# Two linked feed-forward layers after attention: the groups of the first layer alternate between two parts of the tokens, and its weights are used for both parts from one load

## The chip, the cores and the metric

The kernel is one program on one core of a Trainium2 chip. The metric is the time of one execution on the device in microseconds (us). TensorE does the matrix products, VectorE, ScalarE and GpSimd the work on single elements, and SyncE (with ScalarE's queue) starts the transfers between HBM and the on-chip memory. In the profile these engines are PE, DVE, ACT, POOL and SP; PEld is TensorE's loading of weights, and ACTq and SPq are transfers that ScalarE and SyncE start.

## The reference

```python
B, H, S, D = 4, 8, 576, 64                # 2304 tokens of 512 columns after attention
# attention with a causal softmax, mixed by a gate with a linear memory (not touched by the change)
x = attn_out.transpose(0, 2, 1, 3).reshape(B * S, H * D)
h = x @ moe_w_in                          # 512 -> 2048
x = np.maximum(0.01 * h, h) @ moe_w_out   # 2048 -> 512
a, b = x @ moe2_w_a, x @ moe2_w_b         # 512 -> 1536, twice
out = (a * b) @ moe2_w_out                # 1536 -> 512
```

All inputs and the result are 32-bit floats, and the weights reach the kernel as 64-bit words that it turns into 32-bit values by integer and float operations on VectorE.

## The kernel before

**Products.** Each matrix factor is kept as a high and a low half (`hi`, `lo`, two tiles of reduced-precision floats whose sum is the value), and each product is made of three matmuls: hi·hi, hi·lo and lo·hi (`three`, lines 393 to 395). The common unit is a matmul of 128x128 weights with 512 columns.

**The first layer.** The 2304 tokens are in two parts: part 0 has 1024 (two chunks of 512 columns), part 1 has 1280 (chunks of 512, 512 and 256). The 2048 hidden columns are in eight groups of 256. For a group g, `inward` computes the hidden values: for each chunk and each half f of the group a block of 12 matmuls into a bank of PSUM (ring `u`, four banks), then ScalarE applies the leaky ReLU into a buffer `gf` (line 1099) and casts it to the high half of a gate tile (1063), and GpSimd subtracts to get the low half (1064). `outward` multiplies the gate tiles of a set of groups with the output weights, four blocks per chunk (ring `o`, four banks); for the first set ScalarE copies the result to the running sum `xf` (line 1115), for later sets VectorE adds it (line 1117). A set of one group has 6 matmuls in a block of `outward`, a set of two has 12.

**The order of the sets.** Group 0 is done for both parts, then the sets [1,2], [3,4], [5,6], [7] of part 0, and then [1,2], [3,4], [5], [6,7] of part 1. All engines run in the order in which the program is written; `after(k, ...)` puts an operation k blocks later, `tick` counts the blocks.

**Weights.** The class `Weights` converts 68 items of 512 columns: 32 "own" items (two for each of the 16 weight tiles of the first layer), then 24 "plain" items and 12 "last" items of the second layer. Four own items are done during attention, 64 during the first layer. An item is loaded by SyncE (`wraw`, line 178), ScalarE takes the absolute value (line 261), VectorE does the steps of lines 292, 293, 302, 303, 307, and for an own item ScalarE casts the high half (299) and VectorE makes the low half (314, 315); a plain or last item ends with one sum (322 or 330) and is written to HBM by SyncE. `convert` sets the pace: so many quarters of an item for each block of matmuls. Converted tiles live in five slots (`RING`). Part 0 uses each tile once and frees it; each own tile is therefore also written to HBM (`kept`, line 318, started by ScalarE) and 14 are read back for part 1 (line 361, started by ScalarE).

**The last 256 tokens of part 1** as halves (`xt`) lie in the tile that later holds a gate; they are written to HBM once (`xkept`) and read back once.

**The second layer** (`moe2`) makes its products from sums of blocks with seven products (1, 6, 5, 7, 2, 3, 4 in `slots`) instead of eight, and `result` (line 1421) multiplies with the output weights and lets VectorE add. At the end of part 0 the sums of part 1's input (`Sums.jobs`, lines 1177 and 1189) are made between the last products.

Of the kernel before, what the change touches and what calls it, by code (L numbers as in the profile page):

```python
# [11 lines left out]
F32 = mybir.dt.float32  # L12
# [105 lines left out]
def attention_moe_moe2(ctx: ExitStack, tc, kqT, qn, vn, m_prev, beta, w_in, w_out, w_a, w_b, w_o2, out):  # L118
# [38 lines left out]
    class Weights:  # L157


        def __init__(self, first, ab, last):  # L160
            self.sources = {"own": first, "plain": ab, "last": last}
            self.pool = None
            self.own = self.n = self.top = self.quarter = self.freed = self.got = 0
# [94 lines left out]
        def absolute(self, n):  # L258

            t = self.abs[n] = {x: self.temp(n, [P, WC], F32, "w" + x) for x in "har"}  # L260
            nc.scalar.activation(t["h"], self.raw[n][:, :, 1].bitcast(F32), AF.Abs)  # L261
# [22 lines left out]
        def quarters(self, n, item):  # L284
# [25 lines left out]
            def four():  # L310
                if n + 1 in self.items:
                    self.absolute(n + 1)
                if kind == "own":
                    V.tensor_tensor(t["a"], t["a"], f32(self.tiles[i][:, 0, c]), ALU.subtract)
                    V.tensor_tensor(self.tiles[i][:, 1, c], t["a"], t["h"], ALU.add)  # L315
                    if part:
                        w = f32(self.tiles[i]).rearrange("p s c -> p (s c)")
                        after(2, lambda: nc.scalar.dma_start(self.kept[i], w))
                    self.done.add(item)
                elif kind == "plain":  # L320
                    k = "p (k f c) -> p f k c"
                    V.tensor_tensor(
                        t["r"].rearrange("p (f k c) -> p f k c", f=2, k=2), t["a"].rearrange(k, k=2, f=2),
                        t["h"].rearrange(k, k=2, f=2), ALU.add,
                    )

                    nc.sync.dma_start(self.plain[i][:, part], t["r"])
                    self.done.add(item)
                else:
                    V.tensor_tensor(t["r"], t["a"], t["h"], ALU.add)  # L330
                    nc.sync.dma_start(self.saved[i][:, part], t["r"])
# [18 lines left out]
        def get(self):  # L350
            i = self.got
            if i < 16:
                self.until("own", i)
            self.got += 3 if i == 15 else 1
            return self.tiles.pop(i)
# [8 lines left out]
        def free(self):  # L364
            self.freed += 3 if self.freed == 15 else 1
            self.fetch()
# [11 lines left out]
    FIRST_SETS = [[1, 2], [3, 4], [5, 6], [7]]  # L378
# [741 lines left out]
    def moe1(ps, pr, sets, x, y):  # L1120
        for groups in sets:
# [5 lines left out]
            for g in groups:  # L1127
                weights.free()
# [499 lines left out]
```

## Time and profile before

| what | value |
| --- | --- |
| time, median of 3 runs | 1033.75 us (1029.85, 1033.75, 1033.86) |
| profiled execution | 1029.21 us, span 1027.4 us, mean granted clock 0.992 |
| PE busy | 997.3 us, 97% of the span |
| DVE busy | 805.7 us, 78% |
| ACT busy | 422.3 us, 41% |
| POOL busy | 402.7 us, 39% |
| HBM read and written | 111.15 MB and 55.05 MB |

Attention ends at about 195 us after the start of the span, the first layer at about 588 us, and the second layer's part 0 at about 790 us. A busy PE includes the time in which a matmul is only draining, so the place to look for lost time is where the step from one matmul's start to the next grows.

### The profile page before, as it was taken

The page shows a single profiled execution, that of the slowest core. Times are in us where ns is not written, and L with a number is a line of the kernel's source. Part 1 is how long each engine was busy: PE and PEld are TensorE (multiplying, and loading weights), DVE is VectorE, ACT ScalarE, POOL GpSimd, SP SyncE. Part 2 cuts the span into 40 slices and gives each one's busy share as a digit, 9 for nine tenths or more (in the row PEclk, how much of TensorE's full clock was granted, in tenths as well). Part 3 has the DMA queues.
Part 4 walks back from the last instruction along what each step waited for, and adds up shares of the span by engine and source line. Part 5 has one row for each costly group of instructions (what it writes and reads, how often), then busy time and mean ns, then how long its engine had stood idle before and what let it go on. Part 6 is the DMA issues. An engine that isn't in the chain of part 4 may idle for free.

```text
span 1027.4 us, 14691 instructions
## 1 busy us (share of the span) xinstructions
PE 997.3 (97%) x5266; PEld 800.8 (78%) x5266; DVE 805.7 (78%) x1520; ACT 422.3 (41%) x947; POOL 402.7 (39%) x371
## 2 busy tenths in 40 slices
PE   9999999999999899999999999999997999999998
PEld 4666667787878688788888878878875888888887
DVE  6999998698999989799987396797787627647646
ACT  7988886665342422415134144332232222201201
POOL 6787777333141412505034366766643101001000
PEclk9999999999999899999999999999998999999999
DMA  7334531155446468667673235456564432332312
GB/s 235 107 119 137 169 114 48 63 171 207 175 163 224 160 206 314 223 211 260 209 262 103 103 123 215 161 199 225 202 215 156 144 133 93 137 141 93 140 46 103
DMA packets 49273, 167.16 MB, mean 163 GB/s; under 512 B 5168, under 2 KB 12080, under 8 KB 40752
## 3 DMA queue, kind: packets, MB, share of 16 engines
q1 hardware_dynamic: 45024, 136.86, 38.9%
q10 hardware_dynamic: 4176, 29.37, 7.7%
q8 instruction: 41, 0.67, 0.3%
q14 instruction: 32, 0.26, 0.1%
HBM read 111.15 MB, written 55.05 MB: 162 GB/s over the span
## 4 chain that ended last, share of the span: by engine, by line
PE 70%; DVE 21%; DMA 5%; ACT 2%; issue 2%; POOL 0%; ACTq 0%; DVEq 0%; SPq 0%; POOLq 0%
PE b L393 19%; PE b L395 19%; PE b L394 19%; PE b L744 4%; PE b L823 4%; PE b L685 3%; DMA wraw<-in_w_b 3%; DVE wh L292 2%; DVE wa L302 2%; DVE w L315 2%; DVE wh L307 2%; DVE xf L1117 2%; DVE wh L303 1%; PE b L795 1%; DVE xs L1189 1%
## 5 line engine op out<-in xcount | busy, mean ns | idle before, releaser
L1359 DVE TENSOR_TENSOR gf<-b,gf 128x512 f32<-128x512 f32 x168 | 114.2, 687 | 72.0 <-PE b L395 67.3
L1421 DVE TENSOR_TENSOR xf<-b,xf 128x512 f32<-128x512 f32 (+1 forms) x91 | 61.8, 682 | 61.7 <-PE b L395 61.5
L375 POOL TENSOR_TENSOR w<-w 128x512 fp32r<-128x512 f32 x24 | 35.3, 1471 | 188.6 <-ACT w L374 188.2
L1064 POOL TENSOR_TENSOR hl<-gf,hl 128x512 fp32r<-128x512 f32 (+1 forms) x37 | 53.3, 1454 | 136.9 <-ACT hl L1063 125.7
L393 PE MATMUL b<-xh,w 128*128 128x512 f32 x256 | 101.7, 397 | 2.4 <-ACT gf L1099 2.4
L394 PE MATMUL b<-xh,w 128*128 128x512 f32 x256 | 100.5, 392 | 0.0
L395 PE MATMUL b<-xh,w 128*128 128x512 f32 x256 | 100.2, 392 | 0.0
L261 ACT ACTIVATE wh<-wraw 128x512 f32<-128x512 f32 x64 | 42.9, 671 | 97.4 <-DMA wraw<-in_w_o 32.4
L393 PE MATMUL b<-xs,bhi 128*128 128x512 f32 (+1 forms) x216 | 79.4, 368 | 2.7 <-DVE gf L1359 2.7
L393 PE MATMUL b<-xs,ahi 128*128 128x512 f32 (+1 forms) x216 | 79.1, 366 | 1.6 <-DVE gf L1359 1.6
L394 PE MATMUL b<-xs,bhi 128*128 128x512 f32 (+1 forms) x216 | 79.2, 367 | 0.2 <-DVE xs L1189 0.2
L394 PE MATMUL b<-xs,ahi 128*128 128x512 f32 (+1 forms) x216 | 79.0, 366 | 0.0
L395 PE MATMUL b<-xs,blo 128*128 128x512 f32 (+1 forms) x216 | 79.0, 366 | 0.0
L395 PE MATMUL b<-xs,alo 128*128 128x512 f32 (+1 forms) x216 | 78.9, 365 | 0.0
L639 ACT ACTIVATE p<-p,stat 128x512 f32<-128x512 f32 (+3 forms) x128 | 71.0, 559 | 5.3 <-DVE stat L693 4.9
L1117 DVE TENSOR_TENSOR xf<-b,xf 128x512 f32<-128x512 f32 (+1 forms) x80 | 50.1, 630 | 25.0 <-PE b L395 25.0
L666 POOL TENSOR_SCALAR p<-p,stat,keep 128x128 f32<-128x128 f32 (+3 forms) x95 | 61.0, 655 | 16.9 <-DVE stat L654 8.6
L1064 POOL TENSOR_TENSOR qs<-gf,qs 128x512 fp32r<-128x512 f32 (+1 forms) x21 | 28.8, 1370 | 92.7 <-ACT qs L1063 72.0
L393 PE MATMUL b<-w,hl 128*128 128x512 f32 (+1 forms) x146 | 57.1, 391 | 7.6 <-DVE xf L1421 7.6
L693 DVE CUSTOM_DVE_ANT_0 p<-b,mask 128x512 f32<-128x512 f32 (+3 forms) x128 | 57.4, 477 | 6.1 <-PE b L685 5.6
L393 PE MATMUL b<-hl,w 128*128 128x512 f32 (+1 forms) x164 | 61.6, 375 | 0.1
L394 PE MATMUL b<-hl,w 128*128 128x512 f32 (+1 forms) x164 | 61.3, 374 | 0.0
(201 smaller groups left out, 2726.1 us busy)
## 6 DMA issues: line engine op xcount, KB each, us to landing
kept<-w ACTq DMA_DIRECT2D x14, 1024.0 KB, 4.3
w<-kept ACTq DMA_DIRECT2D x14, 1024.0 KB, 5.3
wraw<-in_w_in SPq DMA_DIRECT2D x16, 512.0 KB, 3.6
wraw<-in_w_out SPq DMA_DIRECT2D x16, 512.0 KB, 3.7
qraw<-in_qn SPq DMA_DIRECT2D x8, 768.0 KB, 6.9
wraw<-in_w_b SPq DMA_DIRECT2D x12, 512.0 KB, 4.3
plain<-wr SPq DMA_DIRECT2D x24, 256.0 KB, 4.6
wraw<-in_w_a SPq DMA_DIRECT2D x12, 512.0 KB, 5.3
```

Source lines behind the costliest of these rows:

```text
L261: nc.scalar.activation(t["h"], self.raw[n][:, :, 1].bitcast(F32), AF.Abs)
L393: nc.tensor.matmul(outp, l_hi, r_hi, start=start, stop=False)
L394: nc.tensor.matmul(outp, l_hi, r_lo, start=False, stop=False)
L395: nc.tensor.matmul(outp, l_lo, r_hi, start=False, stop=stop)
L639: nc.scalar.activation(t, t, AF.Exp, bias=s[:, 0, col : col + 1], scale=-1.0, accum_out=s[:, 1, col : col + 1])
L666: ENG[eng].tensor_scalar(live[p], live[p], stats[w % 3][:, 3, col : col + 1], k, ALU.mult, ALU.mult)
L693: nc.vector.tensor_tensor_reduce(one(p, [P, wd]), plan.tiles[banks[j]][:, c : c + wd], mask[:, off : off + wd], -0.125, BIG, ALU.add, ALU. ...
L744: nc.tensor.transpose(tt[0:kw, n * 128 : n * 128 + 128], live[name][:, kt * 128 : kt * 128 + kw], ident)
L1064: after(1 if eng is nc.vector else 2, lambda: eng.tensor_tensor(t[:, 1, c], gf, f32(t)[:, 0, c], ALU.subtract))
L1117: nc.vector.tensor_tensor(y[:, dm, c], op[:, 0:n], y[:, dm, c], ALU.add)
L1359: nc.vector.tensor_tensor(left[q, to], src, left[q, add], ALU.add)
L1421: nc.vector.tensor_tensor(y[:, i, c], op, y[:, i, c], ALU.add)
```

## The change

The sets become one list, `SETS`, in which parts alternate and each part lags or leads by one group: part 0 [0], part 1 [0,1], part 0 [1,2], part 1 [2,3], part 0 [3,4], part 1 [4,5], part 0 [5,6], part 0 [7], part 1 [6,7]. A weight tile stays in its slot until both parts have used it (`used`), so nothing of it is written to HBM or read back. Part 1 has four sets instead of five. In `inward` the low half for f = 1 is made by VectorE instead of GpSimd, with the number of operations the same. The fourth gate tile of a part-1 set holds the last 256 tokens' halves in its first 1024 columns until the set's second group has used them (its chunks come in the order 2, 0, 1), so these are read back from `xkept` at the start of the sets 3, 5 and 8. The plain and last items are summed in place (`wa`), in plain order; the second layer takes its blocks from that order (`columns`, `pair`). In `slots`, the last column pair of part 0 gets the same mixed order as the others, and four sums of part 1's input are put behind its last product.

```diff
-            self.kept = [dram.tile([P, 4 * WC], F32, tag=f"kept{i}", name=f"kept{i}") for i in range(16)]
...
                     V.tensor_tensor(self.tiles[i][:, 1, c], t["a"], t["h"], ALU.add)
-                    if part:
-                        w = f32(self.tiles[i]).rearrange("p s c -> p (s c)")
-                        after(2, lambda: nc.scalar.dma_start(self.kept[i], w))
                     self.done.add(item)
                 elif kind == "plain":
...
-                    nc.sync.dma_start(self.plain[i][:, part], t["r"])
+                    V.tensor_tensor(t["a"], t["a"], t["h"], ALU.add)
+                    nc.sync.dma_start(self.plain[i][:, part], t["a"])
...
-        def fetch(self):
-            while self.asked < min(32, self.freed + RING):
-                i = self.asked
-                t = f32(self.tile(i)).rearrange("p s c -> p (s c)")
-                after(2, lambda t=t, i=i: nc.scalar.dma_start(t, self.kept[self.again[i - 18]]))
-                self.asked += 1
...
+        def used(self, i):
+            self.uses[i] += 1
+            if self.uses[i] == 2:
+                self.tiles.pop(i)
+                self.freed = i + 1
...
-    FIRST_SETS = [[1, 2], [3, 4], [5, 6], [7]]
-    SECOND_SETS = [[1, 2], [3, 4], [5], [6, 7]]
+    SETS = [(0, [0]), (1, [0, 1]), (0, [1, 2]), (1, [2, 3]), (0, [3, 4]), (1, [4, 5]), (0, [5, 6]), (0, [7]), (1, [6, 7])]
...
-                halves(t, c, gf, nc.gpsimd)
+                halves(t, c, gf, nc.vector if f else nc.gpsimd)
...
+    def moe1(ps, first, fourth, x, y):
+        for n, (pr, groups) in enumerate(SETS):
             gt = []
+            t3 = fourth(n) if pr or len(groups) > 1 else None
+            for j, g in enumerate(groups):
+                if n == 0:
+                    gt += first
+                else:
+                    ts = [shared("qs0"), t3] if j else [shared("hl0"), shared("hl1")]
+                    gt += ts
+                    cs = chunks(pr)
+                    wi = weights.get(2 * g)
+                    for kind, w in inward(ps, pr, g, wi, x[pr], ts, cs[2:] + cs[:2] if j else cs):
+                        yield n, kind, g, w
+                weights.used(2 * g)
+            wos = [weights.get(2 * g + 1) for g in groups]
+            for kind, w in outward(ps, pr, groups[-1], wos, gt, y(pr), n < 2):
+                yield n, kind, groups[-1], w
...
-                text = ("16572O3O4OO", "1657234OOOO" if g == 5 else "1O6O5OO7234")[a] if g else "1657234"
+                text = ("16572O3O4OO", "1O6O5OO7234")[a] if g else "1657234"
...
+                if n > 1:
+                    nc.sync.dma_start(f32(t)[:, :, 0:1024], xkept)
...
+            convert(w, 0.7 if n == 0 else 0.74)
...
-                jobs += [steps[x] for x in {"1": "1b", "6": "6", "5": "5", "7": "7c", "2": "2", "3": "3", "4": "4"}[k]]
+                jobs += [steps[x] for x in {"1": "1b", "6": "6", "5": "5", "4": "7c234"}.get(k, "")]
```

How the order of instructions moves, at three places. The first is ScalarE where part 1 follows part 0, before: the names are a gate tile (`qs`, `xs`), `gf` the leaky ReLU, `wh` the absolute value of a loaded item, `w<-kept` a weight read back.

```order
L1099 ACTIVATE gf_4391<-b_4378 128x512
L261 ACTIVATE wh<-wraw 128x512
L361 DMA w<-kept_76 128x2048
L361 DMA w<-kept_77 128x2048
L361 DMA w<-kept_78 128x2048
L1063 CAST qs_4377<-gf_4391 128x512
L1099 ACTIVATE gf_4421<-b_4408 128x512
L1063 CAST xs_4275<-gf_4421 128x512
L1099 ACTIVATE gf_4442<-b_4429 128x512
L261 ACTIVATE wh<-wraw 128x512
L1063 CAST qs_4377<-gf_4442 128x512
```

And ScalarE at the start of a part-1 set now (`hl` is a gate tile, lines 1077 and 1043 are the leaky ReLU and the cast).

```order
L1077 ACTIVATE gf_4489<-b_4476 128x512
L261 ACTIVATE wh<-wraw 128x512
L1043 CAST hl_4474<-gf_4489 128x512
L1077 ACTIVATE gf_4512<-b_4499 128x512
L1043 CAST hl_4475<-gf_4512 128x512
L1077 ACTIVATE gf_4535<-b_4522 128x512
L261 ACTIVATE wh<-wraw 128x512
L1043 CAST hl_4474<-gf_4535 128x512
```

No transfer is started by ScalarE any more; the waits for loaded items (line 261) still stand ahead of the leaky ReLUs. The second place is VectorE in the `inward` part of the set 3 now: one plain item and the subtraction that GpSimd did before (line 1044).

```order
L292 TENSOR_SCALAR wh<-wh 128x512
L293 TENSOR_SCALAR wa<-wh 128x512
L302 SCALAR_TENSOR_TENSOR wa<-wraw,wa 128x512
L303 TENSOR_SCALAR wh<-wa 128x512
L307 SCALAR_TENSOR_TENSOR wh<-wraw,wh 128x512
L1044 TENSOR_TENSOR hl_3618<-gf_3655,hl_3618 128x512
L318 TENSOR_TENSOR wa<-wa,wh 128x512
```

Each item of about two blocks now has one such subtraction in the middle of it. The third place is VectorE at the end of the second layer's part 0, from product 3 of the last pair on. Before:

```order
L1359 TENSOR_TENSOR gf<-b_7422,gf 128x512
L1386 TENSOR_TENSOR gf<-gf 128x512
L1177 TENSOR_TENSOR raw<-xf,raw 128x512 x2
L1359 TENSOR_TENSOR gf<-b_7435,gf 128x512
L1386 TENSOR_TENSOR gf<-gf 128x512
L1344 TENSOR_TENSOR hl_7400<-gf,hl_7400 128x512
L1421 TENSOR_TENSOR xf<-b_7452,xf 128x512
L1189 TENSOR_TENSOR xs_4275<-raw,xs_4275 128x512 x2
L1421 TENSOR_TENSOR xf<-b_7465,xf 128x512
```

And now, from the first product's sum on (1419 is the addition of an output block, 1357 a sum of products, 1384 the product of the two columns, 1342 the low half of a gate, 1166 and 1178 the sums of part 1's input and their low halves).

```order
L1419 TENSOR_TENSOR xf<-b_7225,xf 128x512
L1166 TENSOR_TENSOR raw<-xf 128x512 x2
L1357 TENSOR_TENSOR gf<-b_7235,gf 128x512
L1178 TENSOR_TENSOR xs_5890<-raw,xs_5890 128x512 x2
L1419 TENSOR_TENSOR xf<-b_7247,xf 128x512
L1357 TENSOR_TENSOR gf<-b_7255,gf 128x512
L1178 TENSOR_TENSOR xs_5890<-xf,xs_5890 128x512 x2
L1419 TENSOR_TENSOR xf<-b_7267,xf 128x512
L1419 TENSOR_TENSOR xf<-b_7275,xf 128x512
```

The four additions of the group before the last stood behind all sums and gates of the last group; now they stand between its first products, and the low half of the last group's gate (1342) is now followed by six sums of part 1's input, four of which stood ahead of it.

## Rows read from the trace of the kernel before

**Rows 1.** The page, busy time of each engine over the span.
```profile
PE 997.3 (97%) x5266; PEld 800.8 (78%) x5266; DVE 805.7 (78%) x1520; ACT 422.3 (41%) x947; POOL 402.7 (39%) x371
```

**Rows 2.** Stretches: length, busy us and instructions by engine, clock, DMA share, GB/s.
```profile
195.00:575.00 380.00, 369.11 (x1759) 308.60 (x1756) 329.02 (x493) 152.07 (x282) 121.98 (x87) 0.99 0.58 198
...
560.00:580.00 20.00, 20.00 (x101) 17.02 (x100) 2.08 (x3) 8.09 (x16) 13.79 (x11) 1.00 0.33 122
...
755.00:790.00 35.00, 25.74 (x106) 20.11 (x105) 29.96 (x35) 10.67 (x17) 14.18 (x8) 0.90 0.58 212
```

**Rows 3.** PE in order of time: start, length, instruction, [idle before <-releaser].
```profile
302.78 0.49 PE L393 MATMUL b<-g,w 128*128 128x512 f32 x1
...
305.39 0.39 PE L393 MATMUL b<-hl,w 128*128 128x512 f32 x1
...
348.12 0.49 PE L395 MATMUL b<-qs,w 128*128 128x512 f32 x1
352.33 0.79 PE L393 MATMUL b<-g,w 128*128 128x512 f32 x1 [3.72 <-ACT w L299]
...
354.79 0.63 PE L393 MATMUL b<-hl,w 128*128 128x512 f32 x1
355.22 0.63 PE L394 MATMUL b<-hl,w 128*128 128x512 f32 x1
...
413.54 0.39 PE L394 MATMUL b<-xh,w 128*128 128x512 f32 x1
413.76 0.39 PE L395 MATMUL b<-xh,w 128*128 128x512 f32 x1
416.55 0.64 PE L393 MATMUL b<-xh,w 128*128 128x512 f32 x1 [2.40 <-ACT gf L1099]
```

**Rows 4.** PE's waits from 195 to 575 us: total us, times, longest.
```profile
PE b L393 <- DVE xf L1117: 1.5, 3, 0.7
PE b L393 <- ACT xf L1115: 1.3, 1, 1.3
```

**Rows 5.** ACT and its queue around 403 to 415 us, in order of time.
```profile
403.16 1.29 ACTq L361 DMA_DIRECT2D w<-kept  x3
...
414.83 0.66 ACT L261 ACTIVATE wh<-wraw 128x512 f32<-128x512 f32 x1 [8.06 <-DMA wraw<-in_w_b]
```

**Rows 6.** Transfers: count, KB each, median us from issue to landing.
```profile
w<-kept ACTq DMA_DIRECT2D x14, 1024.0 KB, 5.3
...
plain<-wr SPq DMA_DIRECT2D x24, 256.0 KB, 4.6
...
xs<-xkept SPq DMA_DIRECT2D x1, 1024.0 KB, 8.6
```

**Rows 7.** DVE in order of time, from 215 to 232 us.
```profile
215.12 1.67 DVE L315 TENSOR_TENSOR w<-wa,wh 128x512 fp32r<-128x512 f32 x1
216.71 1.51 DVE L292 TENSOR_SCALAR wh<-wh 128x512 f32<-128x512 f32 x1
...
222.83 0.96 DVE L292 TENSOR_SCALAR wh<-wh 128x512 f32<-128x512 f32 x1
...
227.82 0.42 DVE L292 TENSOR_SCALAR wh<-wh 128x512 f32<-128x512 f32 x1
...
231.25 0.69 DVE L315 TENSOR_TENSOR w<-wa,wh 128x512 fp32r<-128x512 f32 x1
```

**Rows 8.** Groups by line, engine and tiles: count, busy us, mean ns, idle before.
```profile
L1064 POOL TENSOR_TENSOR hl<-gf,hl 128x512 fp32r<-128x512 f32 x30 | 45.8, 1536 | 136.5 <-ACT hl L1063 125.2 <-issue 7.8 <-DVE wh L307 2.3
...
L1099 ACT ACTIVATE gf<-b 128x512 f32<-128x512 f32 x60 | 35.7, 595 | 40.8 <-PE b L395 37.1 <-POOL hl L1064 1.7 <-DVE w L315 1.6
...
L1344 DVE TENSOR_TENSOR hl<-gf,hl 128x512 fp32r<-128x512 f32 x20 | 22.4, 1119 | 0.0
```

**Rows 9.** PE where part 1 of the first layer begins.
```profile
206.34 0.39 PE L393 MATMUL b<-xh,w 128*128 128x512 f32 x1
```

**Rows 10.** PE at the end of the second layer's part 0.
```profile
772.55 0.39 PE L395 MATMUL b<-w,hl 128*128 128x512 f32 x1
779.10 0.76 PE L393 MATMUL b<-w,hl 128*128 128x512 f32 x1 [6.16 <-DVE xf L1421]
```

**Rows 11.** DVE at the same place.
```profile
775.51 2.84 DVE L1344 TENSOR_TENSOR hl<-gf,hl 128x512 fp32r<-128x512 f32 x1
778.27 0.68 DVE L1421 TENSOR_TENSOR xf<-b,xf 128x512 f32<-128x512 f32 x1
```

More of the change, by code (lines that the diff above doesn't have):

```diff
@@ L385, in attention_moe_moe2 @@
     )
-    weights.again = [names.index(x) for s in SECOND_SETS for x in [("in", g) for g in s] + [("out", g) for g in s]]
-    weights.asked = 18
     xf = {}
@@ L1470, in x_of @@
         def x_of(s, kt, c):
[L1471 removed]
+            return t3s[0][:, s, kt * 256 : kt * 256 + 256] if c.start >= 1024 else x1[:, s, kt, c]
         def piece(kt, c, eng):
@@ L1486, in attention_moe_moe2 @@
-        weights.free()
-        nc.sync.dma_start(xkept, f32(t))
-        y1 = part_tile(main, "xf", 1)
-        for kind, g, w in outward(ps, 1, 0, [w1], gt, y1, True):
-            convert(w, 0.8)
-        weights.free()
-        gtags.append(lambda: sb.tile([P, 2048], F32R, tag="g3", bufs=1, name="g3"))
-        n = 0
-        weights.spare += [("plain", m, h) for m in range(12) for h in range(2)] + [("last", g, h) for g in range(6) for h in range(2)]
-        for kind, g, w in moe1(ps, 0, FIRST_SETS, lambda s, kt, c: x0[:, s, kt, c], y0):
-            if (kind, g) == ("o", 7) and n == 0:
-                n = 1
-                sums.first()
-                xts[0] = sums.tail
-                nc.sync.dma_start(f32(sums.t1)[:, 0:2048], xkept)
-            convert(w, 0.8 if kind == "u" else 0.74)
@@ new lines, in y @@
+        def y(pr):
+            if pr not in ys:
+                ys[pr] = part_tile(main, "xf", pr)
+            return ys[pr]
+        t31 = fourth(1)
+        jobs += [lambda kt=kt, c=c: piece(kt, c, (nc.vector, nc.gpsimd)[kt % 2]) for c in chunks(1) for kt in range(4)]
+        weights.spare += [("plain", m, h) for m in range(12) for h in range(2)] + [("last", g, h) for g in range(6) for h in range(2)]
+        m = 0
+        xs = [lambda s, kt, c: x0[:, s, kt, c], x_of]
+        for n, kind, g, w in moe1(ps, gates, lambda n: t31 if n == 1 else fourth(n), xs, y):
+            if n == 1 and m == 0:
+                m = 1
+                nc.sync.dma_start(xkept, f32(t31)[:, :, 0:1024])
+            if n == len(SETS) - 1:
+                if (kind, g) == ("u", 6) and m == 1:
+                    m = 2
+                    raw = sb.tile([P, 2 * WIDE], F32, tag="g3", bufs=1, name="raw")
+                    mats = Matrices(raw[:, 0:2048])
+                    mats.load(0)
+                    mats.when = now[0]
+                if (kind, g) == ("u", 7) and m == 2:
+                    m = 3
+                    jobs.append(sums.jobs(ys[0], None)["1"])
+                    mats.make(0)
+                if kind == "o":
+                    m += 1
+                if m == 9:
+                    m = 10
+                    while weights.items or weights.quarter or weights.spare:
+                        weights.step()
+                        tick()
+                    spares = [main.tile([P, 512], F32, tag=f"gf{i}", bufs=1, name="gf") for i in range(3)]
+                    t = main.tile([P, 2 * WC], F32, tag="wraw", bufs=1, name="gf")
+                    spares += [t[:, 0:WC], t[:, WC : 2 * WC]]
+                    spares += [main.tile([P, WC], F32, tag=k, bufs=1, name="gf") for k in ("wh", "wa", "wr")]
+                    sums.second()
+                    steps = sums.jobs(ys[0], {f"S{i + 1}": spares[i * 2 : i * 2 + 2] for i in range(4)})
+                    jobs += [steps[k] for k in "ab65c2d7"]
+                    mats.make(1)
+            run(2)
+            convert(w, 0.7 if n == 0 else 0.74)
```

132 lines of the change are left out of this document (45 added, 87 removed).

## The prediction

> **What bounds the kernel now.** I read the busy times first: TensorE is busy 97% of the span, VectorE 78%, GpSimd 39% [rows 1]. The number of matmuls doesn't change, so the change can only win back time in which TensorE steps more slowly than its own pace. That pace is the step between two starts in an undisturbed stretch, 413.54 to 413.76, about 0.227 us for a matmul of 512 columns [rows 3]. Wherever a step is longer, time is lost. So next I read TensorE in order of time, with the cause beside each gap.
>
> Between 195 and 575 us, nearly all of the first layer, VectorE is busy 329 of 380 us [rows 2], and I find these losses:
> - 302.78 to 305.39: three steps take 2.61 us instead of 0.68, a loss of 1.9 [rows 3]. GpSimd's low half and VectorE's last operation on an own weight are late.
> - 348.12 to 354.79: four steps take 6.67 us instead of 0.91, so 5.8; ScalarE's cast of an own weight is late. Then the steps are 0.43 us (354.79 to 355.22), TensorE at the lower of its two clock levels, 1.2 GHz, for nine steps at 0.2 us more: 1.8. Together 7.6 [rows 3].
> - 413.76 to 416.55: 2.79 instead of 0.23, so 2.6, again with some nine slow steps, 1.8; together 4.4 [rows 3].
> - ScalarE's copies at 232 us, 1.3 idle with the restart 1.5, and three waits for VectorE's sums near 531 to 541 us, 1.5 idle, which I read with restarts as 2.5 [rows 4].
>
> The sum is 18 us. In the second layer one place is as bad: from 755 to 790 us only 106 matmuls start in 35 us; at 0.227 they need 24, so 11 us are lost, 6.3 of it in the one gap at 772.55, and the clock of the stretch is 0.90 [rows 2, 10].
>
> **The change, part by part.**
>
> *Own weights at half the rate of demand.* Before, part 0 takes 14 tiles within some 180 us and VectorE converts them back to back; beside GpSimd one item takes 6.1 us (216.71 to 222.83), with GpSimd idle 4.1 (227.82 to the end of the operation at 231.25) [rows 7]. Two blocks of matmuls last 24 x 0.227 = 5.44 us. That is why the deadlines at 302 and 348 were missed. Now a tile serves both parts, and a slot is free one set before its next tile is needed: from set 2 on the loading of a tile may start one part-0 set (16 blocks of 2.72 us, 43.5) and some blocks more before its first matmul, and its two items cost VectorE 8 to 12 us. Both stalls should go: minus 9.5.
>
> *No write and no reading back.* 14 transfers of 1 MB leave and as many return [rows 6]. The stall at 413 hangs on them: three read-backs start at 403.16, and ScalarE stands for 8.06 us in front of an absolute value whose load comes late; the leaky ReLUs that empty TensorE's banks are behind it [rows 5]. Without these transfers the load comes in time: minus 4.4.
>
> *Set of two instead of one in part 1.* The copies at 232 and the sums at 531 come at one in 1.36 us, because a block of a single-group set has 6 matmuls. Part 1 has no such set any more; the blocks have 12. Both stalls go: minus 4. One set less also saves VectorE 12 sums; at 0.68 us for 512 columns [rows 11] and some 0.4 for the four narrower ones that is about 7 us of its time, not of the span. The set [7] of part 0 stays single: 8 sums and 8 quarters of an item in 10.9 us fit into the four banks' delay.
>
> *Half of the low halves from GpSimd to VectorE.* Of the 60 blocks of 512 columns [rows 8], 30 move, and 8 narrow ones. A subtraction of this kind takes VectorE 1.12 us in the second layer beside GpSimd [rows 8], and 0.69 is what its like takes undisturbed [rows 7]: between 24 and 39 us more on VectorE. GpSimd's operation takes 1.54 [rows 8]. While it runs, VectorE's take longer: an item costs 6.1 instead of 4.1, that is 2 us for two GpSimd operations. 38 of these less give back up to 38 us; I take two thirds, 26, since not all of them fall beside VectorE's work. VectorE's load comes to 329 - 7 - 26 + (24 to 39) = 320 to 335 us in a stage that shrinks to about 362. So it stays just under full, and I take it as hidden. If that cover is gone, each microsecond of surplus is paid by TensorE.
>
> The Trainium skill, "Perfetto Trace Analysis", section "Optimizing Scalar/DVE Operations", says that GpSimd and VectorE share a read port into the on-chip memory and that moving operations between these two might therefore not help. The trace agrees that they delay each other. By the rule alone the swap would be worth nothing; by the rows the sum of the two engines falls. What it would do here if it holds in full is the second rival.
>
> *First sets.* Group 1's weights of the input side are now needed by part 1's second group, at 206.34 + 5 x 2.72 = 219.9 us [rows 9], where before an `outward` of the same 13.6 us stood between. VectorE finished them at 216.8 [rows 7]. 3 us of slack, less one or two subtractions: I count nothing, with 0 to 2 as bounds.
>
> *Reading back the last tokens.* At the start of the sets 3 and 5 SyncE waits until TensorE has ended the set before, then fetches 1 MB; behind it in the queue stand a store and the next load of a weight item, and VectorE waits for those. The one such transfer took 8.6 us [rows 6]; TensorE reaches the tile after four blocks, 10.9 us. It is hidden with 2 us to spare. If VectorE is late by as much, the load ahead of it in the queue is late too: 0 to 3 us for each of two sets. The sums in place give a store of 4.6 us [rows 6] only about one item of time (5.4 us) before its buffer is written again; that costs VectorE an occasional microsecond. For all these new waits I take 2.5 us, with 0 and 8 as bounds.
>
> *The end of part 0 in the second layer.* The four additions move in front of the last products, so the banks come free, and the gap then ends with the last gate's low half (775.51 to 778.35 [rows 11]). From the last pair's first product on, VectorE has to do about 20 operations before that: with the durations of the trace, contended ones as they stand, 20.4 us from 2.9 us after the start on; if the two longest (this one and a product of 1.8 us) come at 0.7 to 1.1, 17.5. TensorE's products and additions last 15.6 up to the same point. So 4.8 to 7.7 are lost, with slow clock behind about 7 in place of 11: minus 4, bounds 2 and 6.
>
> Other edits (the order of the plain items, the other places for tiles) move transfers of the same size or larger pieces and no order on TensorE: nothing.
>
> The sum is -9.5 - 4.4 - 4 + 2.5 - 4 = -19.4 us against the profiled execution's 1029.2: 1009.8. That execution is at the fast end of the runs shown, 1029.85 to 1033.86 with the median 1033.75; against the median it is 1014.4. I predict 1012, between the two.
>
> **The rivals.**
> - *The waits come back in part.* VectorE runs nearly full, and new waits (read-back, first sets, late low halves) cost 8 instead of 2.5, each with slow clock behind it, and the second layer's place wins only 2: -18 + 8 - 2 = -12, or 1017 to 1022. For it: the busy 329 of 380 before, in-place stores, SyncE's wait. Against: the deadlines move by tens of microseconds.
> - *VectorE becomes the bound, and the kernel slower.* If GpSimd's halved work gives nothing back, two blocks of `inward` ask 5.7 us for an average item (6.1 for an own one, less for a plain one) plus 1.12 for the subtraction, 1.4 more than the 5.44 that TensorE gives. There are 34 such pairs: 47 us; pairs of `outward` with two sums recover about 14. 33 us lost against the 22 won: 1029 + 11 to 1034 + 11, about 1042. It decides from a relief below 0.3 us for each of the 38 operations taken off GpSimd (33 - 11 = 22). The contended and clean items in the same stage speak against it.
> - *Nothing that shows.* The losses at 302 to 358 us are VectorE's total and not its deadlines; they would then spread over the first layer as short waits for sums and low halves, and only the read-backs' 4.4 would be won, of which the new waits take 2.5: 1027 to 1032. Against: before, VectorE works only 2 of the 20 us from 560 to 580 [rows 2], so its total leaves slack at the end.
>
> **How the numbers follow.** I give the forecast 0.64, waits coming back in part 0.2, nothing that shows 0.09, the slower case 0.07. The likeliest alone lies between 1004 (all won, no new wait, from the profiled time) and 1018. The range that leaves out about 2 in 10 reaches up into the first rival: 1004 to 1024. A measurement of this kernel tells about 0.5%, 5 us. Faster than 1028.6: the forecast, the first rival and a part of the third, 0.86; the same 0.08; slower 0.06.
>
> **What would show it.** Right: no wait of TensorE over 1 us between 240 and 560 us, the clock at 1.00 there; no transfers on ScalarE's queue; loads of weight items never near 10 us; GpSimd's line with half the count and VectorE's new subtraction between 0.69 and 1.12; VectorE's busy time in the first layer within 320 to 335; the gap at the end of part 0 still there, 5 to 7 us, ended by a low half and not by an addition. Wrong: steps of 0.43 us in the first layer; TensorE waiting for a read-back (`xkept`) in set 3 or 5, or for the new subtraction at each start of `outward`; VectorE without idle time up to the end of the first layer.

## The result

| | before | after |
| --- | --- | --- |
| median | 1032.33 us (4 runs, 1029.85 to 1033.86) | 1018.83 us (4 runs, 1017.84 to 1019.85) |
| profiled execution | 1029.21 us, span 1027.4, clock 0.992 | 1017.84 us, span 1016.1, clock 0.998 |

The ratio is 0.987, with a 95% interval of 0.985 to 0.990: the change makes the kernel 13.5 us faster by the medians, 11.3 by the spans of the two profiled executions. Forecast were 1012 with 1004 to 1024, and 19.4 us. The range holds the time, but the likeliest case promised too much.

The page of the changed kernel, busy time of each engine, stands against [rows 1]:

```profile
PE 991.3 (98%) x5266; PEld 798.7 (79%) x5266; DVE 804.8 (79%) x1546; ACT 424.2 (42%) x947; POOL 351.0 (35%) x333
```

GpSimd loses 52 us, VectorE stays the same in total. The stretches of the changed kernel (length, busy us and instructions by engine, clock, DMA share, GB/s):

```profile
195.00:575.00 380.00, 374.94 (x1810) 316.25 (x1807) 326.63 (x523) 153.58 (x283) 70.24 (x50) 1.00 0.41 133
575.00:610.00 35.00, 32.11 (x165) 27.41 (x164) 31.09 (x47) 13.43 (x23) 18.03 (x12) 1.00 0.39 143
610.00:755.00 145.00, 139.42 (x611) 113.81 (x610) 112.50 (x157) 48.49 (x84) 90.60 (x63) 1.00 0.50 182
755.00:790.00 35.00, 30.89 (x144) 24.64 (x143) 28.66 (x37) 11.83 (x20) 16.42 (x9) 1.00 0.57 208
```

Against [rows 2], TensorE's busy time in the first layer has risen by 6 us, and in the last stretch 144 matmuls start where 106 did. But from 610 to 755 TensorE is idle for 5.6 us, in a stretch in which the kernel before was idle for 1.2:

```profile
610.00:755.00 145.00, 143.80 (x634) 118.41 (x633) 112.24 (x167) 51.02 (x90) 97.41 (x68) 1.00 0.53 195
```

To see where time is lost I add up, for each step from one matmul's start to the next, what it takes beyond the undisturbed 0.4427 ns for each column (0.227 us for 512), leaving out excesses of less than 0.02 us. From 195 us to the end ("all" also has what is lost behind 795, 0.2 in both):

| us lost by TensorE | 195 to 575 | 575 to 610 | 610 to 750 | 750 to 795 | all |
| --- | --- | --- | --- | --- | --- |
| before | 18.5 | 2.9 | 1.8 | 11.3 | 34.6 |
| after | 7.8 | 3.2 | 6.8 | 5.3 | 23.1 |

The difference, 11.5, is that of the spans within 0.2. So nothing else counts in sum, and each experiment below is read by the same sums. TensorE's waits of the changed kernel from 195 us on (total us, times, longest):

```profile
PE b L373 <- DVE gf L1357: 5.1, 2, 3.1
PE b L374 <- DVE xs L1044: 3.7, 1, 3.7
PE b L373 <- DVE xf L1095: 2.9, 1, 2.9
PE b L373 <- DVE xf L1419: 1.4, 1, 1.4
PE b L375 <- POOL qs L1342: 1.4, 1, 1.4
PE b L373 <- ACT qs L1340: 1.1, 1, 1.1
PE b L373 <- ACT gf L1077: 0.7, 1, 0.7
PE b L373 <- DMA g<-xkept: 0.6, 1, 0.6
```

All the waits of [rows 3, 4] are gone. Two things are new: the wait for L1044 (the subtraction moved to VectorE) and those for the read-back. There are two of these: the list puts one down to ScalarE (0.7, L1077), but it too ends with the first matmul that reads the tile `g`, and e6 below takes both away. Waits for sums of products in the second layer (L1357) were there before (as L1359, the longest 1.6 us), but none of 3 us. Here are the first two places on TensorE, in order of time:

```profile
555.76 0.39 PE L373 MATMUL b<-xs,w 128*128 128x512 f32 x1
559.83 0.80 PE L374 MATMUL b<-xs,w 128*128 128x512 f32 x1 [3.68 <-DVE xs L1044]
560.42 0.63 PE L375 MATMUL b<-xs,w 128*128 128x512 f32 x1
560.85 0.63 PE L373 MATMUL b<-hl,w 128*128 128x512 f32 x1
...
649.72 0.39 PE L375 MATMUL b<-w,qs 128*128 128x512 f32 x1
653.23 0.50 PE L373 MATMUL b<-xs,bhi 128*128 128x512 f32 x1 [3.12 <-DVE gf L1357]
```

At 555.76 the wait costs 3.8, and the slow steps behind it, most of them of 0.43 as from 560.42 to 560.85, another 1.7: 5.5 of the 7.8 us of the first layer. What VectorE did before it:

```profile
543.36 2.63 DVE L1044 TENSOR_TENSOR hl<-gf,hl 128x256 fp32r<-128x256 f32 x1
545.92 1.22 DVE L307 SCALAR_TENSOR_TENSOR wh<-wraw,wh 128x512 f32<-128x512 uint32 x1
547.06 3.61 DVE L1257 TENSOR_TENSOR raw<-raw 128x256 f32<-128x256 f32 x4
...
552.63 1.51 DVE L292 TENSOR_SCALAR wh<-wh 128x512 f32<-128x512 f32 x1
554.18 1.40 DVE L293 TENSOR_SCALAR wa<-wh 128x512 uint32<-128x512 uint32 x1
555.62 1.64 DVE L302 SCALAR_TENSOR_TENSOR wa<-wraw,wa 128x512 uint32<-128x512 uint32 x1
...
559.09 1.28 DVE L1044 TENSOR_TENSOR xs<-gf,xs 128x512 fp32r<-128x512 f32 x2
```

VectorE works without a pause from 540 to 560, on items, low halves and the second layer's first sums (L1257), and GpSimd works beside it (543.06 to 556.72, idle for 1.0 of it). L292, L293 and L302 take 1.4 to 1.6 us here; where GpSimd is idle, they take 0.42, 0.43 and 0.69 in this trace. The two subtractions for which TensorE waits are last in the queue.

At 649 us it is the sums again. VectorE and then GpSimd, after:

```profile
645.58 6.27 DVE L1257 TENSOR_TENSOR raw<-raw 128x256 f32<-128x256 f32 x4
651.77 1.40 DVE L1357 TENSOR_TENSOR gf<-b,gf 128x512 f32<-128x512 f32 x2
...
644.90 2.40 POOL L1145 TENSOR_TENSOR xs<-xf,xs 128x1024 fp32r<-128x1024 f32 x1
647.25 4.32 POOL L1264 TENSOR_TENSOR alo<-raw,ahi 128x512 fp32r<-128x512 f32 x3
```

And the same place of the kernel before:

```profile
655.87 3.13 DVE L1259 TENSOR_TENSOR raw<-raw 128x256 f32<-128x256 f32 x4
...
655.19 2.39 POOL L1156 TENSOR_TENSOR xs<-xf,xs 128x1024 fp32r<-128x1024 f32 x1
658.64 5.27 POOL L1266 TENSOR_TENSOR alo<-raw,ahi 128x512 fp32r<-128x512 f32 x4 [1.06 <-ACT ahi L1262]
```

Before, GpSimd's low halves of the matrix start at 658.64, when VectorE's four sums are nearly done. Now three of them run beside the sums, which take twice as long.

### The profile page after: what moved, and what is told of

It reads as the page before. It is cut to its first block, busy times and chain, and to the rows that moved or that the text cites. A ratio compares the mean times of both kernels' runs of the same rounds, so it can differ in the third digit from the quotient of the medians.

```text
span 1016.1 us, 14584 instructions
## 1 busy us (share of the span) xinstructions
PE 991.3 (98%) x5266; PEld 798.7 (79%) x5266; DVE 804.8 (79%) x1546; ACT 424.2 (42%) x947; POOL 351.0 (35%) x333
## 5 line engine op out<-in xcount | busy, mean ns | idle before, releaser
L1357 DVE TENSOR_TENSOR gf<-b,gf 128x512 f32<-128x512 f32 x148 | 100.8, 687 | 63.5 <-PE b L375 58.8
L1419 DVE TENSOR_TENSOR xf<-b,xf 128x512 f32<-128x512 f32 (+1 forms) x91 | 61.7, 683 | 60.9 <-PE b L375 60.5
L1044 POOL TENSOR_TENSOR hl<-gf,hl 128x512 fp32r<-128x512 f32 (+1 forms) x20 | 28.3, 1415 | 233.3 <-ACT hl L1043 224.2
L359 POOL TENSOR_TENSOR w<-bhi,w 128x512 fp32r<-128x512 f32 x24 | 35.8, 1492 | 181.2 <-ACT w L358 180.8
L1077 ACT ACTIVATE gf<-b 128x512 f32<-128x512 f32 (+1 forms) x76 | 42.0, 553 | 82.5 <-PE b L375 80.8
L373 PE MATMUL b<-hl,w 128*128 128x512 f32 (+1 forms) x176 | 65.8, 374 | 2.9 <-DVE xf L1095 2.9
L374 PE MATMUL b<-hl,w 128*128 128x512 f32 (+1 forms) x176 | 65.6, 373 | 0.0
L375 PE MATMUL b<-hl,w 128*128 128x512 f32 (+1 forms) x176 | 65.4, 372 | 0.0
L302 DVE SCALAR_TENSOR_TENSOR wa<-wraw,wa 128x512 uint32<-128x512 uint32 x64 | 56.0, 875 | 1.4
```

The costliest lines, as they stand in the source:

```text
L302: V.scalar_tensor_tensor(u["a"], raw[:, :, 1], 0xC0000000, u["a"], ALU.bitwise_and, ALU.bitwise_or)
L359: after(k + 6, lambda f=f: nc.gpsimd.tensor_tensor(w[:, 1, f], f32(stage), f32(w)[:, 0, f], ALU.subtract))
L373: nc.tensor.matmul(outp, l_hi, r_hi, start=start, stop=False)
L374: nc.tensor.matmul(outp, l_hi, r_lo, start=False, stop=False)
L375: nc.tensor.matmul(outp, l_lo, r_hi, start=False, stop=stop)
L1077: nc.scalar.activation(gf, hp[:, 0:n], AF.Prelu, alpha=0.01)
```

## The experiments

**Theories.** **A.** The new loss from 610 to 755 comes from the plain order of the matrices, an edit that the prediction counted at nothing. With blocks and sums interleaved, each piece of 512 columns held some of VectorE's sums, so ScalarE's casts and GpSimd's low halves had to come after the sums. In plain order columns 0 to 1023 hold only loaded blocks; their casts need only the load, and GpSimd works beside the sums. Rivals: the sums' new form (two pieces of 128 columns) is slower by itself, or the other places for tiles are at fault. **B.** The wait at 556 comes from the second layer's work and the last items falling on VectorE and GpSimd together. **C.** The waits for the read-back come from its place in SyncE's queue. For the first layer's gain the question is which part made it: longer deadlines, fewer transfers, or the subtractions taken off GpSimd.

Each stands beside runs of the kernel before on its own chip; the medians of before were 1034.9 (e1 to e4), 1035.6 (e5 to e8) and 1033.2 (e9, e10). Lines and lost time are those of one profiled execution, which can lie some us from the median: 1014.7 in e1, 1028.8 in e2, 1021.7 in e7, 1029.0 in e10.

**e1, the sums first.** Edit to the changed kernel:

```diff
-            for p in range(4):
-                after(k + 1 + p, hi(p))
-                after(k + 2 + p, low(p))
+            for i, p in enumerate((2, 3, 0, 1)):
+                after(k + 1 + i, hi(p))
+                after(k + 2 + i, low(p))
```

> The changed kernel with one edit: the four casts and four low halves of a plain matrix are taken in the order of columns 1024 to 2047 first, then 0 to 1023, so that ScalarE's first cast needs VectorE's four sums of pairs (L1257) again. Theory A: in plain order the casts of the loaded half need only the load, so GpSimd's low halves (L1264) start while VectorE makes the sums, and the sums last 6.27 us for four at 645.58 where the kernel before had 3.13; TensorE's waits at 649.7 (3.3), 680.4 (0.6) and 683.9 (2.2) come from it. Then these waits nearly go, the mean of L1257 falls from 0.675 to about 0.55 us, and the time is 4 to 5 us below the changed kernel's 1018.8, 1013.5 to 1015. Rival B: the strided form of the sums (two pieces of 128 columns instead of 256 in a row) is itself slower on VectorE, or the other places for tiles are at fault: the waits stay, 1018 to 1020.

Measured: 1012.47 us, ratio 0.980 (0.977 to 0.982), 1 us better than theory A's range. The waits at 650 and 680 are gone, and the one behind them costs 1.4 as before. The same place now (VectorE, GpSimd):

```profile
647.44 3.13 DVE L1257 TENSOR_TENSOR raw<-raw 128x256 f32<-128x256 f32 x4
...
650.68 5.07 POOL L1264 TENSOR_TENSOR alo<-raw,ahi 128x512 fp32r<-128x512 f32 x4 [1.52 <-PE b L375]
```

3.13 again, in the strided form, and the sums' mean from 600 us on is 466 ns where the changed kernel had 675: the form is not at fault. Theory A holds, its first rival falls. The wait at 556 stays. The one at 585 falls to 0.3, but two of 0.8 and 0.7 stand behind it, as in the kernel before, so that 575 to 610 loses as much as ever.

**e4, the plain order alone, in the kernel before** (three edits: the item's sum, the load, and the columns of blocks and sums, as in the change).

```diff
-                o, a, b = (raw[:, self.PLACE[n] * 256 : self.PLACE[n] * 256 + 256] for n in (o, a, b))
+                o, a, b = (self.pair(n) for n in (o, a, b))
```

> The kernel before with one part of the change alone: plain items stored and loaded in plain order (the loaded half of a matrix in columns 0 to 1023, the sums in 1024 to 2047, sums of pairs of 128 columns). The prediction counted this edit at nothing. Theory A (see the run with the sums first): GpSimd's low halves now meet VectorE's sums; the mean of L1259 rises from 0.56 to about 0.67 us and TensorE gets waits of 2 to 5 us in all between 610 and 760: 1034 to 1037 beside 1032 of the kernel before. Theory B (other places for tiles, or the room in the raw tile, are at fault): no change, 1031 to 1033.

Measured: 1040.93 us, ratio 1.006 (1.004 to 1.009): this part by itself makes the kernel slower, by 6.0 us beside its chip's 1034.9, where 2 to 5 were expected. The sums' mean rises from 559 to 676 ns (line 1265 here, from 600 us on):

```profile
L1265 DVE TENSOR_TENSOR raw<-raw 128x256 f32<-128x256 f32 x40 | 25.4, 676 | 0.3
```

TensorE loses 8.0 us from 610 to 750 instead of 1.8. The tiles are in their old places here, so the second rival falls too.

**e2, the end of part 0 as before.**

```diff
-                text = ("16572O3O4OO", "1O6O5OO7234")[a] if g else "1657234"
+                text = ("16572O3O4OO", "1657234OOOO" if g == 5 else "1O6O5OO7234")[a] if g else "1657234"
...
-                jobs += [steps[x] for x in {"1": "1b", "6": "6", "5": "5", "4": "7c234"}.get(k, "")]
+                jobs += [steps[x] for x in {"1": "1b", "6": "6", "5": "5", "7": "7c", "2": "2", "3": "3", "4": "4"}[k]]
```

> The changed kernel with the old text of slots for the last pair of part 0 and the old places of the sums of part 1's input. The prediction's term for this edit was minus 4 (2 to 6); the traces show 11.2 us lost from 765 to 780 before and 5.3 now. If the order alone wins this, the time rises by 4 to 6 us to 1023 to 1025, with one gap of about 6 us behind the third product ended by an addition (L1419). If something else of the change made the end quicker (less on VectorE, another contention), it stays at 1018 to 1020.

Measured: 1023.27 us, ratio 0.991 (0.988 to 0.994): 4.4 us above the changed kernel by the medians, as expected. The two intervals overlap a little, so the trace has to decide: from 750 to 795 us 12.9 are lost, against 5.3, and the old wait of 6.2 for an addition (L1419) is back. The order itself wins this.

**e3, all low halves on GpSimd again.**

```diff
-                halves(t, c, gf, nc.vector if f else nc.gpsimd)
+                halves(t, c, gf, nc.gpsimd)
```

> The changed kernel with all low halves of inward on GpSimd again. Theory A: the swap was not needed in the first layer once the deadlines are loose, and the subtraction on VectorE is what TensorE waits for at 555.8 (5.9 us with slow steps): without it this wait goes or shrinks to 1 or 2, and the rest stays, 1013 to 1016; L1043's waiters stay under 1 us elsewhere. Theory B, that of the prediction: beside GpSimd's operations VectorE's items take up to 6.1 us, so VectorE's load grows by some 26 less 24 to 39 us, about nothing, and the first layer stays as it is, 1017 to 1020. Rival C: GpSimd, with 60 operations of 1.54 us and the pieces of the sums, becomes late at the start of each outward, 1022 to 1030.

Measured: 1018.13 us, ratio 0.985 (0.982 to 0.988), the same as the changed kernel. The first layer:

```profile
195.00:575.00 380.00, 376.20 (x1821) 317.14 (x1818) 338.81 (x489) 153.62 (x283) 120.59 (x88) 1.00 0.39 133
```

VectorE has 338.8 us to do with the subtractions on GpSimd and 326.6 with half of them on VectorE itself. The time is theory B's, but not its ground: B expected VectorE's load to stay as it was. The wait at 556 shrinks to 1.7 (for GpSimd now), as A says, and the first layer loses 2.8 us less. But the steps behind 585 us are at the lower clock (575 to 610 at 0.95), which costs 1.6, and 610 to 750 loses 1.4 more; that takes the gain away in this execution. The waits at 302 to 348 don't return.

**e7, that swap alone, in the kernel before** (the same line, with VectorE for f = 1).

> The kernel before with one part of the change alone: the low halves of inward for f = 1 on VectorE. In the changed kernel taking this part back left the time the same while VectorE's busy time from 195 to 575 us rose from 326.6 to 338.8 us. Theory A: VectorE's total falls here too, from 329 to about 317, and with it some of the lateness of the own weights at 302 and 348 us (1.9 and 5.8 us before): 1028 to 1032. Theory B, the swap is worth nothing for the time wherever the deadlines stand: 1031 to 1036. Rival C: beside back-to-back items the subtraction comes late, TensorE waits for it at the start of outward, slower, 1037 to 1043.

Measured: 1025.12 us, ratio 0.990 (0.988 to 0.992), better than all three expectations. VectorE is busy for 322.8 us from 195 to 575, 6 less than before, and TensorE loses 11.2 us there instead of 18.5; the waits left are

```profile
PE b L393 <- DVE xf L1117: 2.3, 3, 1.9
PE b L393 <- ACT gf L1099: 1.8, 2, 1.6
PE b L393 <- ACT w L299: 1.2, 1, 1.2
PE b L395 <- DVE w L315: 1.1, 1, 1.1
PE b L393 <- ACT xf L1115: 0.6, 1, 0.6
```

Where deadlines are tight, VectorE's relief is worth time. Three read-backs still start together here (396.13), a load of an item behind them takes 10.1 us (10.5 before), and TensorE still loses 1.9 us at 407, in the place of the old stall at 413.

**e8, the transfers added to the changed kernel.**

```diff
+                    if part and i > 1:
+                        w = f32(self.tiles[i]).rearrange("p s c -> p (s c)")
+                        after(2, lambda: nc.scalar.dma_start(self.kept[i], w))
...
             if self.uses[i] == 2:
+                if i > 1:
+                    after(2, lambda: nc.scalar.dma_start(self.kept2[i], self.kept[i]))
```

> The changed kernel with transfers added: each own weight tile but the first two is written to HBM again as before, and when both parts have used it, a copy of 1 MB from HBM to HBM is started by ScalarE, in the place of the old reading back. Nothing else is changed; the copies are not used. The prediction put the loss at 413 us (4.4) down to these transfers and the losses at 302 and 348 (9.5) to the deadlines. Theory A: with deadlines loosened the transfers cost little, 0 to 2 us, 1018 to 1021, though the loads of weight items take 5 to 10 us where they are 3.3 now. Theory B: the traffic alone makes the loads late, and waits of TensorE for ScalarE's leaky ReLU (L1077) of 2 us and more come back: 1022 to 1028.

Measured: 1023.77 us, ratio 0.990 (0.988 to 0.992), an interval that overlaps the changed kernel's. By the time that is theory B's range, but its waits are absent: none for a leaky ReLU, only 1.4 (listed for a cast, L1050) and 1.0 at the sets 3 and 5, where 0.6 and 0.7 stood. The sums of lost time differ by 3.5 us: 2.1 in the first layer, and 1.4 in steps at the lower clock behind the wait at 587 us (575 to 610 at 0.95). The transfers cost a little, and don't bring the 4.4 us of 413 back. But they are not placed as the old read-backs were. As many bytes move from 195 to 575 us (205 GB/s, 198 before), yet the copies start at least 10 us apart there, and no load of an item takes more than 6.8 us. Before, three read-backs started together at 403.16, and the load behind them took 10.5. A burst of three was not tried in the changed kernel.

**e10, both of these: the sets alone are left in the first layer** (the edits of e3 and e8 together).

> The changed kernel with two parts taken back in the first layer: all low halves of inward on GpSimd again (as in e3), and the writing of each tile with a copy of 1 MB in the place of each reading back (as in e8; the copies are not used). What is left in the first layer are the new sets with one use of a tile by both parts, so this shows what the longer time for each tile is worth by itself. e7 showed that the swap alone wins some 7 us in the first layer of the kernel before. Theory A: the deadlines by themselves are enough: no wait of TensorE over 1.5 us between 230 and 540 us, and the time stays at that of e8 and e3, 1019 to 1025. Theory B: swap and transfers are the real causes and the sets only hide behind them: waits for own weights (ScalarE's cast L299 or VectorE's L315, two lines or so further down here) near 300 to 350 us or for late loads come back, 8 us or more in all, 1027 to 1034.

Measured: 1026.36 us (1019.86 to 1029.49), ratio 0.992 (0.989 to 0.995). Neither theory as written:

```profile
PE b L380 <- DMA g<-xkept: 6.4, 2, 3.4
PE b L380 <- DVE gf L1364: 5.2, 2, 3.1
PE b L380 <- DVE xf L1102: 2.9, 1, 2.9
```

No wait for an own weight comes back, so the new sets by themselves cure 302 and 348. None for a late load does either, but as in e8 no burst of three is there to cause one. The read-back, late already, now costs 3.4 and 3.0 us in the sets 3 and 5. (About 1.5 of the 13.4 us that the table below has for e10's first layer are still attention's, which ends 3 us later in this execution.)

**e6, the read-back started by ScalarE** (on e1).

```diff
-                    nc.sync.dma_start(f32(t)[:, :, 0:1024], xkept)
+                    nc.scalar.dma_start(f32(t)[:, :, 0:1024], xkept)
```

> The kernel with the sums first (e1), with the read-back of the last tokens (xkept) started by ScalarE instead of SyncE. In e1 TensorE begins set 3 at about 305 us, but SyncE starts the read-back at 308.2, behind a load of a weight item that waits for its buffer; it lands 8.7 us later, and TensorE waits 0.9 and 1.1 us at 315.7 and 415.5. Theory A: the late start in SyncE's queue is the cause; started by ScalarE the transfer begins at 305 to 306, both waits go, 2 to 2.5 us less, 1010 to 1011. Rival B: the transfer itself is slower beside the loads, or ScalarE's queue now delays leaky ReLUs while it waits for TensorE: 1012 to 1015, with waits for ScalarE (L1077) at the start of the sets 3, 5 and 8.

Measured: 1009.46 us, ratio 0.976 (0.974 to 0.978). SyncE's queue in the changed kernel and ScalarE's in e6:

```profile
308.12 0.33 SPq L178 DMA_DIRECT2D wraw<-in_w_b  x1
308.50 0.57 SPq L1469 DMA_DIRECT2D g<-xkept  x1
```

```profile
305.87 0.59 ACTq L1469 DMA_DIRECT2D g<-xkept  x1
308.54 0.60 ACT L1077 ACTIVATE gf<-b 128x512 f32<-128x512 f32 x1 [6.66 <-PE b L375]
```

It starts 2.6 us earlier, and in 5.3 instead of 8.4 us it has landed; both waits are gone, and ScalarE was idle there. Theory C holds. The lost time of the first layer falls by 7.0 against e1, but the two waits are only 2.5 of it; the rest is at 556, where the wait is 2.3 instead of 4.0 and no steps of 0.43 follow, where e1 has twelve.

**e5, the second layer's first sums later** (on e1).

```diff
-                if (kind, g) == ("u", 7) and m == 2:
+                if kind == "o" and m == 2:
```

> The kernel with the sums first (e1), with one more edit: the first matrix's sums, casts and low halves (make(0)) and the first sums of part 0's output are started at the first block of the last outward instead of at the start of group 7's inward. Theory A: at 543 to 560 us VectorE has in one stretch three converted items, the new subtractions (L1044), the sums and GpSimd's nine operations beside all of them; the last two subtractions come at 560 and TensorE waits 4.2 us at 556.3 with slow steps behind. Without the second layer's work there the subtractions come in time: that wait falls below 1.5 us, and the time is 3 to 5 us below e1's 1012.5, 1007 to 1010. Rival B: VectorE's items alone keep it too late, the wait stays above 3 us, 1011 to 1014. Rival C: the work meets the sums of outward from 560 on and the gap at 587 grows by as much, 1011 to 1015.

Measured: 1054.24 us, ratio 1.019 (1.017 to 1.021), outside every expectation. The wait at 556 is gone, as A says: from 195 to 575 us 2.7 are lost, 2.2 of it at the sets 3 and 5. But TensorE waits for every later matrix:

```profile
PE b L375 <- POOL blo L1264: 20.0, 5, 4.2
PE b L373 <- ACT bhi L1260: 9.2, 5, 4.2
PE b L375 <- POOL alo L1264: 4.8, 5, 1.3
```

The first cast of a matrix stands at 559.6 us instead of 548.9 in e1. By the code, `make` sets each matrix some ticks behind the last one (`when`), so that a delay is handed on; that this is all of it was not tried. 30.8 us are lost from 610 to 750, and 6.1 behind 795. Starting this work early is worth much more than the wait that it causes.

**e9, the items moved instead** (on e6).

```diff
-            convert(w, 0.7 if n == 0 else 0.74)
+            last = n == len(SETS) - 1
+            if not (last and (kind, g) == ("u", 7)):
+                convert(w, 0.7 if n == 0 else 1.0 if last and kind == "o" else 0.74)
```

> The kernel with the sums first and the read-back started by ScalarE (e6), with one edit: during group 7's inward of the last set no item is converted; the last one and a half items follow during the last outward. In e5 the wait at 556 was gone when the second layer's first sums were moved away, but they became late for all that follows. Theory A: it is the sum of VectorE's items and GpSimd's operations that makes the last subtractions (L1044) late; with the items moved instead, the wait of 2.5 us at 554 in e6 falls below 0.8, nothing behind becomes late, and the time is 2 to 3 us below e6's 1009.5: 1006.5 to 1008. Rival B: GpSimd's own queue (nine operations from 543 to 557) decides, and the wait stays with GpSimd (L1044) as its end, 1009 to 1011. Rival C: the items come late for the second layer's output weights or the buffers that it takes over (wraw, wh, wa), and a wait near 590 grows: 1010 to 1014.

Measured: 1004.98 us (1004.81 to 1005.43), ratio 0.972 (0.970 to 0.975), the fastest of all and 1.5 us better than expected. The wait at 556 is gone with the items, so B holds with the items as the half that can move. The first layer:

```profile
195.00:575.00 380.00, 380.00 (x1848) 321.70 (x1845) 331.72 (x535) 155.86 (x288) 70.28 (x50) 1.00 0.39 133
```

The lost time of all runs, worked out as above (us; behind 795 it is 6.1 in e5, 0.7 in e4 and 0.2 in the others):

| | 195 to 575 | 575 to 610 | 610 to 750 | 750 to 795 | all |
| --- | --- | --- | --- | --- | --- |
| e1 | 10.1 | 3.1 | 1.8 | 5.3 | 20.3 |
| e2 | 10.1 | 4.7 | 6.7 | 12.9 | 34.5 |
| e3 | 5.0 | 4.7 | 8.2 | 5.2 | 23.3 |
| e4 | 20.3 | 4.7 | 8.0 | 11.1 | 44.8 |
| e5 | 2.7 | 10.0 | 30.8 | 9.3 | 58.8 |
| e6 | 3.1 | 3.1 | 1.8 | 5.3 | 13.4 |
| e7 | 11.2 | 2.9 | 1.8 | 10.6 | 26.6 |
| e8 | 9.9 | 4.6 | 6.8 | 5.2 | 26.6 |
| e9 | 0.4 | 3.0 | 1.8 | 5.3 | 10.6 |
| e10 | 13.4 | 5.9 | 8.1 | 5.4 | 33.0 |

## Why the prediction was right, and where not

The time fell into the range and on the forecast side of the chances, but at 1018.8 into the band of the first rival (1017 to 1022). That rival named the right sort of cause, waits that come back, and two of the right places, the late low halves and the read-back; its 8 us for them are near the 7.8 measured. That its whole sum came out is luck: it gave the second layer's end 4 us too little (2, measured 6) and did not see 5 lost by the plain order, and the two errors cancel. By steps:

- **Own weights (9.5): right.** Both stalls are gone, also without the swap (e3) and without swap and saved transfers (e10).
- **No write and reading back (4.4): the gain is there, its ground stays open.** With the transfers back, but one by one (e8, e10), the stall at 413 doesn't return, so it wasn't the bytes alone. The prediction's own ground was three read-backs starting together ahead of a load. In the kernel before, with VectorE relieved and the burst left (e7), 1.9 us of the stall remain, which speaks for the burst; that tight deadlines are needed with it is not shown. What shows of the transfers in e8 and e10 is a later read-back.
- **No single-group set in part 1 (4): right.** No waits for L1093 or L1095 between 195 and 575.
- **Low halves on VectorE, "I take it as hidden": the step failed at one place.** The load was right (326.6, forecast 320 to 335; subtractions of 512 columns at 0.69). It is a sum over 380 us, and it says nothing of the last 20, where GpSimd is busy for the second layer: there the cover is gone, at 5.5 us. "No wait over 1 us between 240 and 560" was wrong at 555.76 alone, and two of the prediction's signs of being wrong are there: steps of 0.43 us behind this wait, and waits for the read-back. And the prediction saw the swap as a cost to hide, not as a second cure of the same stalls: by itself it wins 7.3 us of the first layer's losses (e7), and beside the new sets nothing (e3). The gains of the two don't add.
- **Reading back and new waits (2.5, bounds 0 to 8):** without 556, 2.3 us are lost in the first layer, 1.9 of it at the sets 3 and 5. "Hidden with 2 us to spare" was wrong: the transfer started 3 us into the set.
- **The end of part 0 (4, bounds 2 to 6): right, at its upper bound.** 6.0 won. The sign that went with it was wrong: a gap of 5 to 7 us, ended by a low half. The one gap of [rows 10] has become four of 0.2 to 1.4 us; two end with a low half (L1342), but the last still with an addition (L1419, 1.4).
- **"Other edits: nothing": this step failed.** The order of the plain items cost 5.0 us from 610 to 750 (e1, and e4 from the other side). The prediction followed what it moves on TensorE and in transfers, and not which operations it sets free to run beside each other.

Together: 19.4 forecast, less 5.2 in the first layer (7.8 lost where 2.6 should have been), 5.0 for the plain order and 0.3 from 575 to 610, plus 2.0 at the end of part 0, plus 0.5 (the losses before 575 were 18.5, not 18): 11.4, and 11.5 are measured.

The prediction set a rule of the Trainium skill ("Perfetto Trace Analysis", section "Optimizing Scalar/DVE Operations") against its rows: moving operations between GpSimd and VectorE might not help. In the changed kernel the trace agrees as to the time (e3), not as to the load: GpSimd gives up 50 us and VectorE has 12 less to do, with the subtractions added. In the kernel before the same move did help, by 10.5 us (e7).

## What to carry to other kernels

A change of layout also changes which operations wait for which. Where two engines slow each other, an order that data forces may be what keeps them apart, so write down for each edit what is freed to start earlier, and beside what. A load that fits a stage as a whole has to be asked again for the last stretch, where the next stage's first work joins it. Two cures for one stall don't add; each has to be taken back by itself to see which one is worth keeping.

## What was not expected of the hardware

- The slowing beside GpSimd is not the same for all VectorE operations. Operations that read and write the on-chip memory alone can stretch to the length of GpSimd's, those of two operands as well as the short ones of one (L292, 1.51 us at 552.63 and 0.42 elsewhere): a subtraction of 256 columns took 2.63 us at 543.36 while GpSimd's operation of 1024 columns ran for 2.64 (from 543.06), and 0.42 is what it takes undisturbed. Sums that read a bank of PSUM (L1357, L1359) have the same mean of 687 ns before and after: in either kernel 685 ns for the 69 that overlap an operation of GpSimd, and 688 for the 99 that don't. The Trainium skill, "SBUF — State Buffer", section "SBUF: two separate sides", describes an exclusive lock of a port pair that VectorE and GpSimd share, held for the whole instruction. On VectorE's side it names operations with two inputs from that memory and those in a two-port fast mode; a sum with one of its inputs in PSUM is neither. These rows agree.
- The same wait can be followed by slow steps or not. At 585 us the changed kernel waits 2.89 us and goes on at its full clock (575 to 610 at 1.00); in e3 a wait of 2.88 for the same operation is in a stretch at 0.95, with 1.6 us more of slow steps, and in e2, e8 and e10 slow steps follow it too. Why one and not the others was not settled.
- The read-back of 1 MB took 5.3 us in e6, where the next load and store started 2.5 and 3.2 us behind it (308.36 and 309.05), and 8.4 in the changed kernel, where a load started 0.4 us ahead of it and a store 0.6 behind (308.12 and 309.13).
